# Attention and a gated feed-forward layer in one kernel: unit pairs in the first weight groups, a split fourth group, and work moved from the vector engine to ScalarE at the start

## The chip, the cores and the metric

The kernel runs on one core of a Trainium2 chip. The metric is the device time of one execution in microseconds. A "slow" or "quick" execution below is a long or short one.

Names that come back: TensorE multiplies matrices (PE in the profile, its weight loads are PEld), the vector engine is DVE, ScalarE is ACT, GpSimd is POOL, and SP issues most of the DMA transfers (95 of 103 in the profile of before, ScalarE the rest).

## The reference

Inputs are `q`, `k`, `v` of shape (8 batches, 8 heads, 576 rows, 64), `w_in` (512 x 2048), `w_out` (2048 x 512) and `beta` (2048).

```python
q_s = softmax(q, axis=-1)              # over the 64 columns
k_s = softmax(k, axis=2)               # over the 576 rows
kv  = einsum('bhsd,bhse->bhde', k_s, v)
x   = einsum('bhsd,bhde->bhse', q_s, kv)   # then heads side by side: 4608 x 512
h   = x @ w_in                         # 4608 x 2048
g   = h / (1 + exp(-beta * h))
out = g @ w_out                        # 4608 x 512
```

## The kernel before

The 4608 rows are worked off in nine slabs of 512: slabs 0 to 7 are the first 512 rows of a batch each, and slab 8 is gathered from the remaining 64 rows of all batches. A slab has two passes. Pass 1 makes 16 hidden units of 128 columns, each from four matmuls over the input pieces `m`; ScalarE applies Silu. Pass 2 multiplies by the output weights. The short K-V matmuls of the next batch stand between them.

At the start everything comes in at once: q, k, v, then the input weights in four column groups of 512 (`c`), then the output weights in the same staging buffers. The input weights are cast to bf16; the output weights are scaled by 1/beta. In a group of four units, unit `f` takes every fourth column:

```python
HB = (0, 1, 2); OB = (3, 4); MB = (5, 6, 7)          # PSUM banks
def pass1_mm(t, f, m, bk):
    ...
    l = bass.AP(WIN, m * DFF + 512 * (f // 4) + f % 4, [[NM * DFF, 128], [4, 128]])
    mm(PS[bk][:, :], l, x[:, m, :], m == 0, m == NM - 1, ...)
    if m == NM - 1: ...  # Silu on ScalarE: GT[:, f, :]
# ... slab 0
FIRST = (12, 5)
at = by_m(0, 0, 4); ...                    # units 0-3, then 4-7, 8-11: input piece outermost
for g in (4, 8):
    at = by_m(0, g, g + 4)
    for m in range(NM):
        at(m)
for e_ in range(2):
    homes_ek(1, e_, [("win", 2, NM - 1)])  # GpSimd zeroes batch 1's key buffer after group 2's last cast
# ... units 12-15 follow one by one, each needing all four pieces
```

Batch 1's attention is done inside pass 2 of slab 0, at places counted in matmuls:

```python
todo = [(107, lambda: go(t_steps(1, (0, 1), (1,)))),     # transposes, QT copied by the vector engine
        (112, lambda: go(t_steps(1, (2, 3), (2,)))),
        (112.1, lambda: scale_wout(14, 2)),
        (115, lambda: kv_mm(1, 0, 0, 0, D + 1)), (117, kv1),   # ends in KVD, on the vector engine
        (122, lambda: out_now(1, 0, 7, DVE)), ...]             # TensorE needs KVD and QT here
...
exp_q(1, 0, 2); norm_main(1, 0, 1); norm_main(1, 1, 1, POOL); scale_wout(8); exp_q(1, 2, 2); ...
```

The remaining rows of a pair of batches (`QRF`) are loaded with the odd batch, normalised, and turned by a transposing DMA into `QTR`; both are issued by SP. For slabs 2 and up pass 1 cycles through three banks (`HB[f % 3]`).

```python
def load(b):
    load_main("qf", ...); load_k(b); load_v(b)
    if b % 2: load_qrem(b - 1)             # batch 3 brings the remaining rows of batches 2 and 3
# slab 0's end: store(0); load(3)
# slab 1, after pass 1: exp_qr(0); norm_rem(0); tr_dma(0)   -> QTR for batches 0 and 1
# slab 1, pass 2, place 101.5 on: outr_steps(1)             -> TensorE needs QTR
```

The softmax here doesn't subtract the row's maximum and nothing guards it: scores larger than these inputs give would overflow.

## Time and profile before

| | before |
|---|---|
| timed, first three executions | 285.06, 285.56, 286.23 us |
| the profiled execution | 286.38 us, span 284.6 us |
| TensorE busy | 277.9 us, 98% |
| vector engine, ScalarE, GpSimd | 42%, 62%, 14% |

TensorE is busy almost throughout, so only its holes can be saved. The first part of the page has the busy times (share of the span, instructions):

```profile
PE 277.9 (98%) x1585; PEld 138.7 (49%) x1585; DVE 120.3 (42%) x220; ACT 176.3 (62%) x240; POOL 39.0 (14%) x58
```

The timeline of TensorE shows the holes. Its columns are start, length, engine, source line, operation, output and inputs, sizes and count, and in brackets an idle time with what ended it. Most matmuls come from one helper, L366, so the tile names tell them apart.

```profile
13.80 1.02 PE L366 MATMUL PS<-XT,WIN 128*128 128x512 bf16 x4
...
15.53 9.49 PE L366 MATMUL PS<-XT,WIN 128*128 128x512 bf16 x43
25.52 3.66 PE L366 MATMUL PS<-XT,WIN 128*128 128x512 bf16 x15 [0.50 <-DVE WIN L564]
29.02 9.44 PE L366 MATMUL PS<-WOUT,GT 128*128 128x512 bf16 x43
...
41.92 1.24 PE L366 MATMUL PS<-WOUT,GT 128*128 128x512 bf16 x5
44.03 0.39 PE L366 MATMUL PS<-QT,KVD 128*128 128x512 bf16 x1 [0.87 <-DVE KVD L403]
...
60.81 8.37 PE L366 MATMUL PS<-WOUT,GT 128*128 128x512 bf16 x38
69.01 0.25 PE L366 MATMUL PS<-QTR,KVD 128*128 128x64 bf16 x3
```

Matmuls of 512 columns start every 0.216 us where nothing is missing (43 in 9.28 us from 29.02). Between 13.80 and 29.02 there are 66 of them, 14.25 us of work in 15.22 us: hole 1. Five matmuls from 41.92 should hand over at 43.0, but the next one starts at 44.03: hole 2. The brackets alone understate both, because the modelled end of a matmul (0.38 us after its start) overlaps the start of the next one (0.216 us after it). Hole 2 ends with KVD; on the timeline of the vector engine:

```profile
43.36 0.61 DVE L403 TENSOR_TENSOR KVD<-PS,RC 64x128 bf16<-64x128 f32 x2
```

The timeline of the vector engine and of GpSimd shows what makes hole 1: the casts of the fourth group and the memset lie on top of each other. The first line is the end of the third group's casts, which the memset waits for.

```profile
21.96 0.76 DVE L564 CAST WIN<-O2S 128x512 bf16<-128x512 f32 x2 [0.59 <-DMA O2S<-in_moe_w_in_dram]
23.31 2.82 DVE L564 CAST WIN<-O2S 128x512 bf16<-128x512 f32 x4 [0.58 <-DMA O2S<-in_moe_w_in_dram]
22.85 2.33 POOL L236 MEMSET EK<- 64x1152 f32 x2 [6.74 <-DVE WIN L564]
```

The same timeline in a narrower window shows one of those four casts by itself, 1.36 us long:

```profile
24.10 1.36 DVE L564 CAST WIN<-O2S 128x512 bf16<-128x512 f32 x1
```

### The profile page before, as it was taken

The numbers are of one execution on the slowest core, as the hardware profiler recorded it, in microseconds if no ns is written. First come the engines' busy times: TensorE is split into PE (matmuls) and PEld (weight loads), VectorE is DVE, ScalarE is ACT, GpSimd is POOL, SyncE is SP. The second block draws the span as 40 slices with busy tenths as digits, with TensorE's granted clock in tenths as the row PEclk, the third lists the DMA queues.
The fourth block names the chain that finished last, engine by engine and source line by source line (L and its number), as shares of the span: only waits on it lengthen the run. The fifth ranks groups of instructions, "written<-read, shape, count | busy, mean of one in ns | idle before, by whom it ended". The sixth has DMA issues, their size and how long they took to land.

```text
span 284.6 us, 3906 instructions
## 1 busy us (share of the span) xinstructions
PE 277.9 (98%) x1585; PEld 138.7 (49%) x1585; DVE 120.3 (42%) x220; ACT 176.3 (62%) x240; POOL 39.0 (14%) x58
## 2 busy tenths in 40 slices
PE   7899998999999999999999999999999999999995
PEld 3554454445555445544554455444554455445443
DVE  4866797109881248114741564054704300110012
ACT  5977656889977935796479737892660086018500
POOL 6623141306212032100130000000000000000000
PEclk9999999999999999999999999999999999999999
DMA  7999999995998999207980033001600030002022
GB/s 246 371 391 406 391 386 379 325 387 101 281 388 211 377 346 318 57 15 234 379 131 1 0 150 74 0 3 79 160 2 0 0 147 2 0 39 111 0 68 79
DMA packets 41210, 50.07 MB, mean 176 GB/s; under 512 B 20324, under 2 KB 28772, under 8 KB 39784
## 3 DMA queue, kind: packets, MB, share of 16 engines
q1 hardware_dynamic: 40240, 48.77, 53.2%
q10 hardware_dynamic: 952, 1.06, 1.3%
q8 instruction: 12, 0.20, 0.3%
q14 instruction: 6, 0.05, 0.1%
HBM read 36.71 MB, written 9.44 MB: 162 GB/s over the span
## 4 chain that ended last, share of the span: by engine, by line
PE 85%; DVE 5%; DMA 4%; SPq 3%; ACT 1%; issue 0%
PE PS L366 85%; DMA O2S<-in_moe_w_in_dram 4%; DVE WOUT L553 2%; SPq L560 2%; SPq L259 1%; DVE QS L332 1%; DVE WIN L564 1%; DVE EQ L334 1%; ACT L295 0%; DVE QT L384 0%; SPq L249 0%; DVE QI L333 0%; ACT GT L637 0%; ACT EQ L295 0%; DVE KVD L403 0%
## 5 line engine op out<-in xcount | busy, mean ns | idle before, releaser
L637 ACT ACTIVATE GT<-PS,BETA 128x512 bf16<-128x512 f32 x144 | 96.8, 688 | 78.5 <-PE PS L366 78.3
L366 PE MATMUL PS<-XT,WIN 128*128 128x512 bf16 x576 | 133.3, 380 | 0.6 <-DVE WIN L564 0.5
L366 PE MATMUL PS<-WOUT,GT 128*128 128x512 bf16 (+2 forms) x592 | 132.8, 373 | 0.0
L366 PEld LDWEIGHTS PS<-XT,WIN 128*128 128x128 bf16 x576 | 64.4, 113 | 57.8 <-DVE WIN L564 1.4
L366 PEld LDWEIGHTS PS<-WOUT,GT 128*128 128x128 bf16 x592 | 55.2, 98 | 62.0 <-DVE WOUT L553 0.3
L704 DVE COPY O2S<-PS 128x512 f32<-128x512 f32 x33 | 22.7, 687 | 107.7 <-PE PS L366 107.7
L366 PE MATMUL PS<-VB,EK 128*128 128x65 bf16 (+2 forms) x306 | 35.8, 192 | 0.7 <-POOL VB L351 0.4
L351 POOL CAST VB<-VF 128x576 bf16<-128x576 f32 x31 | 23.1, 747 | 75.0 <-DMA VF<-in_v_dram 37.3
L307 ACT ACTIVATE EK<-KF 64x1152 bf16<-64x1152 f32 x24 | 27.8, 1158 | 0.4
L366 PEld LDWEIGHTS PS<-VB,EK 128*128 128x128 bf16 x306 | 22.5, 99 | 8.0 <-POOL VB L351 1.0
L332 DVE TENSOR_REDUCE QS<-EQ 128x8 f32<-128x512 bf16 (+1 forms) x22 | 20.1, 914 | 3.6 <-ACT EQ L295 3.5
L441 DVE CAST XT<-PS 128x512 bf16<-128x512 f32 x24 | 16.4, 690 | 10.9 <-PE PS L366 10.9
L295 ACT ACTIVATE EQ<-QF 128x512 bf16<-128x512 f32 x32 | 17.8, 618 | 2.4 <-DMA QF<-in_q_dram 2.2
L334 DVE TENSOR_TENSOR EQ<-EQ,QI 128x1024 bf16<-128x1024 bf16 (+1 forms) x15 | 16.6, 1104 | 0.5
L366 PE MATMUL PS<-QT,KVD 128*128 128x512 bf16 x32 | 12.2, 380 | 0.9 <-DVE KVD L403 0.9
L317 ACT ACTIVATE EK<-KF 64x576 bf16<-64x576 f32 (+1 forms) x12 | 10.0, 840 | 4.0 <-DMA KF<-in_k_dram 3.9
L334 POOL TENSOR_TENSOR EQ<-EQ,QI 128x512 bf16<-128x512 bf16 x7 | 7.4, 1051 | 23.3 <-DVE QI L333 23.1
L403 DVE TENSOR_TENSOR KVD<-PS,RC 64x64 bf16<-64x64 f32 (+2 forms) x28 | 8.6, 308 | 1.7 <-PE PS L364 0.8
L366 PE MATMUL PS<-XT 128*128 128x512 f32 x10 | 7.5, 883 | 1.5 <-DVE XT L219 1.5
L340 DVE TENSOR_REDUCE QRS<-EQR 128x8 f32<-128x512 bf16 x4 | 2.7, 681 | 13.2 <-ACT EQR L322 13.2
L637 ACT ACT_TABLE_LOAD x5 | 6.4, 1283 | 0.1
L295 ACT ACT_TABLE_LOAD x5 | 6.4, 1283 | 0.1
(51 smaller groups left out, 77.8 us busy)
## 6 DMA issues: line engine op xcount, KB each, us to landing
out_dram<-O2S SPq DMA_DIRECT2D x8, 1024.0 KB, 4.9
KF<-in_k_dram SPq DMA_DIRECT2D x6, 1152.0 KB, 8.5
VF<-in_v_dram SPq DMA_DIRECT2D x6, 1152.0 KB, 11.3
QF<-in_q_dram SPq DMA_DIRECT2D x6, 1024.0 KB, 7.1
KF<-in_k_dram SPq DMA_DIRECT2D x8, 288.0 KB, 8.0
VF<-in_v_dram SPq DMA_DIRECT2D x8, 288.0 KB, 8.8
WST<-in_moe_w_in_dram SPq DMA_DIRECT2D x8, 256.0 KB, 8.1
O2S<-in_moe_w_in_dram SPq DMA_DIRECT2D x4, 512.0 KB, 12.0
```

Source lines behind the costliest of these rows:

```text
L295: add(ACTE, lambda e, o=o, a=a: e.activation(o, a, ACT.Exp), r=[("qf", i, hp)], w=[("eq", i, hp)])
L307: add(ACTE, lambda e, o=o, a=a: e.activation(o, a, ACT.Exp), r=[("kf", i, h) for h in hps], w=[("ek", i, h, e_) for h in hps])
L317: add(ACTE, lambda e: e.activation(o, a, ACT.Exp), r=[("kf", i, h) for h in hps], w=[("ek", i, h, e_) for h in hps])
L332: add(DVE, lambda e: e.tensor_reduce(s_, a, AX.X, ALU.add), r=ks, w=[("qs", i, hp0)])
L334: add(eng, lambda e: e.tensor_tensor(a, a, vb, ALU.mult), r=ks + [("qi", i, hp0)], w=ks)
L351: add(eng, lambda e: (e.copy if eng == ACTE else e.tensor_copy)(o, a), r=[("vf", i, hp), ("vone", i)], w=[("vb", i, hp, h) for h in ((0, 1 ...
L366: add(PE, lambda e: e.matmul(o, l, r_, start=start, stop=stop), r=r, w=w, bank=[bk])
L403: add(DVE, lambda e, o=o, a=a, s_=s_: e.tensor_tensor(o, a, s_, ALU.mult), r=[("ps", bk)] + [("rc", i, h) for h in hps], w=[("kvd", i, h, ...
L441: add(eng, lambda e: (e.copy if eng == ACTE else e.tensor_copy)(XT[i][:, hp, :], PS[bk][:, :]), r=[("ps", bk)], w=[("xt", i, hp)], bank=[bk])
L553: add(DVE, lambda e, f=f: e.tensor_scalar(WOUT[:, f, :], STAGE[f // 4][:, f % 4, :], RB[:, f:f + 1], None, ALU.mult), r=[SKEY[f // 4][f % ...
L637: add(ACTE, lambda e: e.activation(GT[:, f, :], PS[bk][:, :], ACT.Silu, scale=BETA[:, f:f + 1]), r=[("ps", bk), "beta"], w=[("gt", f)], ba ...
L704: add(eng, lambda e: (e.copy if eng == ACTE else e.tensor_copy)(O2S[t % 2][:, u, :], PS[bk][:, :]), r=[("ps", bk)], w=[("o2", t % 2, u)], ...
```

## The change

The intent: close hole 1 by taking the fourth group in pairs of units with the input piece outermost, and by zeroing the key buffer later; close hole 2 by moving two QT copies (and one value cast) to ScalarE; scale the third output-weight group earlier, since TensorE will ask for it earlier; and let the first eight units take every second column instead of every fourth. The core of the diff:

```diff
+            if f < 8:       # load_wout: rows in pairs, to match
+                a = bass.AP(wout_h, 512 * c * DM, [[2 * DM, 128], [256 * DM, 2], [1, 2 * DM]])
+                o = bass.AP(STAGE[c], 0, [[4 * DM, 128], [2 * DM, 2], [1, 2 * DM]])
...          # turn_beta: 8 small transposes instead of 4, to match
-            l = bass.AP(WIN, m * DFF + 512 * (f // 4) + f % 4, [[NM * DFF, 128], [4, 128]])
+            n = 2 if f < 8 else 4
+            l = bass.AP(WIN, m * DFF + 128 * (f // n * n) + f % n, [[NM * DFF, 128], [n, 128]])
...
-        FIRST = (12, 5)
+        FIRST = (16, 5)
...          # head: one input cast from GpSimd to the vector engine, outputs 2 and 3 swap engines
-        for g in (4, 8):
-            at = by_m(0, g, g + 4)
+        for g, n in ((4, 4), (8, 4), (12, 2), (14, 2)):
+            at = by_m(0, g, g + n)
...
-            homes_ek(1, e_, [("win", 2, NM - 1)])
+            homes_ek(1, e_, [("win", 3, NM - 1)])
...
-                todo = [(107, lambda: go(t_steps(1, (0, 1), (1,)))),
-                        (112, lambda: go(t_steps(1, (2, 3), (2,)))),
-                        (112.1, lambda: scale_wout(14, 2)),
+                todo = [(107, lambda: go(t_steps(1, (0, 1), (1,), ACTE))),
+                        (112, lambda: go(t_steps(1, (2, 3), (2,), ACTE))),
+                        (112.1, lambda: (scale_wout(14, 2), exp_kh(1, 2, 1, 0), exp_kh(1, 2, 1, 1))),
...
+                scale_wout(8)
                 norm_main(1, 1, 1, POOL)
-                scale_wout(8)
...
-                    cast_v(1, hp)
+                    cast_v(1, hp, POOL if hp else ACTE)
```

More of the change, by code (lines that the diff above doesn't have):

```diff
@@ L536, in go @@
                 s()
-        load_v(0, 4)
         STAGE = (WST[0], WST[1], O2S[1], O2S[0])
@@ L546, in load_wout @@
             c, x = f // 4, f % 4
-            a = bass.AP(wout_h, (512 * c + x) * DM, [[4 * DM, 128], [1, n * DM]])
-            o = bass.AP(STAGE[c], x * DM, [[4 * DM, 128], [1, n * DM]])
+            if f < 8:
+                a = bass.AP(wout_h, 512 * c * DM, [[2 * DM, 128], [256 * DM, 2], [1, 2 * DM]])
+                o = bass.AP(STAGE[c], 0, [[4 * DM, 128], [2 * DM, 2], [1, 2 * DM]])
+            else:
+                a = bass.AP(wout_h, (512 * c + x) * DM, [[4 * DM, 128], [1, n * DM]])
+                o = bass.AP(STAGE[c], x * DM, [[4 * DM, 128], [1, n * DM]])
             add(SP, lambda e: e.dma_start(o, a), w=SKEY[c][x:x + n], slot=f"wst{f}")
@@ L569, in turn_beta @@
         def turn_beta():
-            for k_ in range(4):
-                mm(bass.AP(PS[KB], 16 + k_, [[512, 128], [4, 4]]),
-                   bass.AP(BT, k_, [[512, 4], [4, 128]]), IDF[0:4, 0:4],
-                   True, True, r=["bt", "idf"], w=[("ps", KB)], bk=KB, tr=True)
+            for g, n, o in ((4, 4, 0), (2, 2, 0), (2, 2, 256)):
+                for k_ in range(n):
+                    mm(bass.AP(PS[KB], 16 + o // 128 + k_, [[512, 128], [4, g]]),
+                       bass.AP(BT, o + k_, [[512, g], [n, 128]]), IDF[0:g, 0:g],
+                       True, True, r=["bt", "idf"], w=[("ps", KB)], bk=KB, tr=True)
         def read_beta():
@@ L606, in bass_efficient_attn_shen__then__act_swish_beta_kernel @@
         ksum(0, 0, KB)
+        load_v(0, 4)
         for c in range(4):
@@ L613, in bass_efficient_attn_shen__then__act_swish_beta_kernel @@
         cast_v(0, 3)
-        for m in range(1, NM):
-            cast_win(0, m, POOL)
+        cast_win(0, 2, POOL)
+        cast_win(0, 3, POOL)
+        cast_win(1, 0, POOL)
         warm(1, 0, True)
@@ L625, in bass_efficient_attn_shen__then__act_swish_beta_kernel @@
         kvd(0, 1, 1, 0)
-        cast_win(0, 0, DVE)
         orot = [0]
@@ L656, in pass1_tile @@
                 tick()
-        FIRST = (12, 5)
+        FIRST = (16, 5)
         out_now(0, 0, 0, ACTE)
+        cast_win(0, 0, DVE)
         kv_mm(0, 2, 7, 0, D + 1)
@@ L662, in bass_efficient_attn_shen__then__act_swish_beta_kernel @@
         kvd(0, 2, 7, 0)
+        cast_win(0, 1, DVE)
         out_now(0, 1, 6, ACTE)
+        at = by_m(0, 0, 4)
         kv_mm(0, 3, 1, 0, D + 1)
+        at(0)
+        out_now(0, 2, 0, ACTE)
         ksum_inv(0, 1, 3, 1, D, 1)
         kvd(0, 3, 1, 0)
-        at = by_m(0, 0, 4)
-        at(0)
-        out_now(0, 2, 0, DVE)
-        at(1, 0, 2)
-        out_now(0, 3, 7, ACTE)
-        at(1, 2)
+        at(1)
+        out_now(0, 3, 7, DVE)
         read_beta()
@@ L678, in bass_efficient_attn_shen__then__act_swish_beta_kernel @@
         for c in range(1, 4):
-            for m in range(NM):
+            for m in range(1 if c == 1 else 0, NM):
                 cast_win(c, m, DVE)
@@ L808, in bass_efficient_attn_shen__then__act_swish_beta_kernel @@
                 exp_kh(1, 0, 2, 1)
-                exp_kh(1, 2, 1, 0)
-                exp_kh(1, 2, 1, 1)
                 norm_main(1, 2, 1, POOL)
```

## The prediction

> **What bounds it now.** TensorE: busy 277.9 of 284.6 us in the profile; 512-column matmuls start every 0.216 us where the timeline is dense (43 in 9.28 us from 29.02). The chain of waits is TensorE alone from 44.03 on. So only TensorE's holes can be saved. After the head (13.8 us) the timeline and the weight-load view show two:
> - Fourth input-weight group, 24.8 to 26.2. From 13.80 to 29.02 there are 66 matmuls, 14.25 us of work in 15.22: 0.97 us lost. Unit 12 needs all four input pieces first, and the vector engine's casts are late: one took 1.36 us instead of 0.42 beside GpSimd's memset of batch 1's key buffer (1.22 us). [...]
> - Batch 1's first output: matmuls resume at 44.03 for a KVD released at 43.98, about 1.0 us lost. The vector engine is busy 9.3 of the 10 us from 30 to 40, and on up to KVD.
>
> DMA is over 90% busy from 3 to 60 us at some 390 GB/s, so loads will not land earlier.
>
> **What the change does.**
> - Fourth group by pairs of units, input outermost: the pieces are wanted at about 24.6, 25.0, 25.5 and 25.9 instead of all within 0.86 us. The memset moves behind the last cast. Estimate: the hole closes, -0.9 us.
> - Two QT copies (1.27 us) leave the vector engine, in the second hole's chain; ScalarE waits 2.5 us for key data before 41.54, so has room. Third-group scales go ahead of batch 1's second normalization: needed, because TensorE would want unit 8 near 34.9, one us earlier. Those weights land near 33.6, so the vector engine may sit 0.7 us, and that normalization is some 1.7 us later; the transposes (wanted near 37.3) and the unit-12 scale (near 39.3) become marginal: up to 0.4 us of new waits. Estimate: KVD near 42.1 instead of 43.98; with the first hole, -1.4 to -1.9 us.
> - First eight units in pairs: column step 2 instead of 4. Weight loads take 113 ns against 98 for unit-step output weights, but hide under 216 ns matmuls: 0. Output-weight loads in 4 KB instead of 8 KB pieces: 0 to +0.2 us in landing, with 0.5 us to spare.
> - Head: one input cast moves from GpSimd to the vector engine, outputs 2 and 3 swap engines, four more small beta transposes: about 0; the pieces' landings (13.2, 13.9, ...) pace it.
>
> Later stages are dense and shift rigidly; ScalarE's exponentials at 62 to 79 us follow, their data having landed.
>
> **Prediction.** 284.0 us against 285.56, range 283.1 to 285.2. Faster by over 2%: 0.01; within 2%: 0.975; slower by over 2%: 0.015.
>
> **What would show it.**
> - First hole: fourth-group casts 0.42 us each, no TensorE wait for WIN, output matmuls starting near 28.1 instead of 29.0.
> - Second: KVD and the first batch-1 output near 42.1, TensorE's wait for KVD under 0.3 us; QT copies about 1 us each on ScalarE, nobody waiting.
> - New waits, if any: transposes on EQ from GpSimd, or unit 12 on WOUT, each under 0.4 us.
> - Pairs: matmul interval unchanged.
>
> **What would make it wrong.** Weights landing later than estimated; the second normalization delaying the transposes by over 1 us; GpSimd casts blocking the fourth scales; ScalarE's added 2.7 us delaying the key exponentials of pair 2, so that the gap moves instead of closing; run-to-run spread (1.2 us before).

The sum came to 284.0 us, 1.56 us under 285.56: -1.4 to -1.9 us for the two holes, 0 for the pairs, 0 to +0.2 us for the landing of the output weights, about 0 for the head. The landing term was the author's estimate and rested on no trace of before; afterwards the two loads in 4 KB pieces landed 11.0 and 11.2 us after their issue in after, beside 11.0 and 11.0 us in before.

## The result, and the profile after

The changed kernel took 285.16 us (median of 6, 284.96 to 285.39) beside 285.35 us for the one before (6 executions, 284.78 to 286.23). The ratio is 0.9992, with a 95% interval of 0.9975 to 1.0009: the same. Ratios are the mean time of one kernel's fast runs over that of the other's of the same rounds, so not quite the ratio of the medians quoted.

The two profiles say something else: the span went from 284.6 to 283.1 us. The profiled execution of before was 286.38 us, slower than all six timed ones; that of after was 284.96 us, its quickest.

Here are the lines of after that answer to those of before: the busy times of the page, then the timeline of TensorE, then that of the vector engine, GpSimd and ScalarE.

```profile
PE 275.2 (97%) x1559; PEld 136.0 (48%) x1589; DVE 117.3 (41%) x218; ACT 178.6 (63%) x243; POOL 38.6 (14%) x57
```

```profile
13.77 1.02 PE L366 MATMUL PS<-XT,WIN 128*128 128x512 bf16 x4
...
28.20 9.44 PE L366 MATMUL PS<-WOUT,GT 128*128 128x512 bf16 x42
...
42.38 0.38 PE L366 MATMUL PS<-QT,KVD 128*128 128x512 bf16 x1
...
59.15 8.36 PE L366 MATMUL PS<-WOUT,GT 128*128 128x512 bf16 x37
68.08 0.26 PE L366 MATMUL PS<-QTR,KVD 128*128 128x64 bf16 x3 [0.57 <-DMA QTR<-EQR]
```

```profile
16.14 0.69 DVE L530 CAST XT<-PS 128x512 bf16<-128x512 f32 x1 [0.64 <-PE PS L366]
...
23.19 0.76 DVE L566 CAST WIN<-O2S 128x512 bf16<-128x512 f32 x2 [0.58 <-DMA O2S<-in_moe_w_in_dram]
24.55 0.76 DVE L566 CAST WIN<-O2S 128x512 bf16<-128x512 f32 x2 [0.60 <-DMA O2S<-in_moe_w_in_dram]
...
41.63 0.61 DVE L403 TENSOR_TENSOR KVD<-PS,RC 64x128 bf16<-64x128 f32 x2
25.43 2.17 POOL L236 MEMSET EK<- 64x1152 f32 x2 [8.68 <-DVE WIN L566]
...
39.74 1.92 ACT L384 COPY QT<-PS 128x1024 bf16<-128x1024 bf16 x2
```

The two holes are closed, but for 0.11 us before batch 1's first output: the casts of the fourth group take 0.43 us each and nobody waits for them, and KVD is done at 42.24 instead of 43.97. A small hole is new, 0.18 us at 16.6. Because outputs 2 and 3 swapped engines, the last input piece of slab 0 is now cast out of PSUM by the vector engine, until 16.83; TensorE could take it up at 16.81 and does so at 16.98. All nine traces of kernels with the changed head show this hole, none of the nine without it. Pass 2 of slab 1 begins 1.66 us earlier (59.15 against 60.81). But nine microseconds later TensorE waits, where it did not before, for the transposing DMA of QTR; only 0.93 us of the 1.66 are left at that point. (Some 30 matmul records are missing in this trace, 1559 against 1589 weight loads; a missing one of 512 columns shows as one start-to-start distance of 0.43 us and is no hole.)

Both traces hold every weight load, so the Nth load from the end can be compared in all of them. The table gives, for each execution that was profiled, its own time and the start of the weight load at four places: the first of slab 0's pass 2 (after hole 1), the first of slab 1's pass 2 (after both holes), the first of slab 2's pass 1 (after QTR), and the last of all. The last column is the distance from the second place to the last.

| execution | its time | slab 0 pass 2 | slab 1 pass 2 | slab 2 pass 1 | last | from slab 1 pass 2 to the last |
|---|---|---|---|---|---|---|
| before | 286.38 | 28.80 | 60.60 | 76.64 | 281.30 | 220.70 |
| before_1 | 284.98 | 28.14 | 59.17 | 75.22 | 279.89 | 220.72 |
| before_2 | 285.43 | 27.86 | 59.58 | 75.63 | 280.31 | 220.73 |
| before_3 | 285.28 | 28.07 | 59.46 | 75.50 | 280.18 | 220.72 |
| before_4 | 286.11 | 28.92 | 60.30 | 76.34 | 281.02 | 220.72 |
| before_5 | 286.64 | 29.06 | 60.85 | 76.90 | 281.56 | 220.71 |
| after | 284.96 | 28.00 | 58.94 | 75.72 | 279.87 | 220.93 |
| after_1 | 284.70 | 27.95 | 58.87 | 75.46 | 279.61 | 220.74 |
| after_2 | 285.04 | 28.02 | 58.93 | 75.81 | 279.96 | 221.03 |
| group4_only | 285.76 | 28.21 | 59.95 | 76.00 | 280.69 | 220.74 |
| act_only | 285.32 | 28.67 | 59.52 | 75.57 | 280.25 | 220.73 |
| pairs_only | 284.71 | 28.07 | 59.31 | 75.36 | 279.62 | 220.31 |
| after_nopairs | 284.73 | 28.07 | 58.92 | 74.97 | 279.66 | 220.74 |
| after_banks | 284.17 | 28.00 | 58.85 | 74.93 | 279.08 | 220.23 |
| qr_late | 284.58 | 28.21 | 59.02 | 75.06 | 279.46 | 220.44 |
| qr_late_2 | 284.44 | 28.07 | 58.92 | 74.97 | 279.37 | 220.45 |
| qr_late_banks | 284.28 | 28.14 | 58.99 | 75.03 | 279.18 | 220.19 |
| qr_late_banks_2 | 284.38 | 28.23 | 59.13 | 75.17 | 279.32 | 220.19 |

Read it by columns. Before runs the last 220.7 us alike to 0.03 us in all six executions; whatever distinguishes a quick execution from a slow one happens before 60 us.

### The profile page after: what moved, and what is told of

The parts are those of the page before. It is cut to its first block, busy times and chain, and to the rows that moved or that the text cites. A ratio compares the mean times of both kernels' runs of the same rounds, so it can differ in the third digit from the quotient of the medians.

```text
span 283.1 us, 3884 instructions
## 1 busy us (share of the span) xinstructions
PE 275.2 (97%) x1559; PEld 136.0 (48%) x1589; DVE 117.3 (41%) x218; ACT 178.6 (63%) x243; POOL 38.6 (14%) x57
## 3 DMA queue, kind: packets, MB, share of 16 engines
q10 hardware_dynamic: 952, 1.06, 1.1%
## 4 chain that ended last, share of the span: by engine, by line
PE 90%; ACT 4%; DMA 3%; issue 1%; DVE 1%; SPq 0%; ACTq 0%
PE PS L366 89%; ACT EK L317 2%; DMA KF<-in_k_dram 2%; DMA QTR<-EQR 2%; ACT L322 0%; SPq L249 0%; PE PS L364 0%; ACT GT L642 0%; DVE QRS L340 0%; DVE EQR L343 0%; ACT VB L351 0%; ACT EQR L322 0%; ACT XT L530 0%; ACT O2S L710 0%; DVE O2S L731 0%
## 5 line engine op out<-in xcount | busy, mean ns | idle before, releaser
L366 PE MATMUL PS<-WOUT,GT 128*128 128x512 bf16 (+2 forms) x579 | 131.4, 373 | 0.7 <-issue 0.2
L366 PE MATMUL PS<-XT,WIN 128*128 128x512 bf16 x561 | 131.2, 379 | 0.5
L366 PEld LDWEIGHTS PS<-XT,WIN 128*128 128x128 bf16 x576 | 60.1, 106 | 59.3 <-POOL WIN L566 0.5
L366 PE MATMUL PS<-QT,KVD 128*128 128x512 bf16 x30 | 11.4, 379 | 0.0
L366 PE MATMUL PS<-XT 128*128 128x512 f32 x10 | 6.7, 801 | 1.5 <-DVE XT L219 1.5
```

The costliest lines, as they stand in the source:

```text
L366: add(PE, lambda e: e.matmul(o, l, r_, start=start, stop=stop), r=r, w=w, bank=[bk])
```

## The experiments

Theories after the first comparison: (A) the profile of before was of a slow execution, so its holes are larger than usual; (B) the holes are constant, and the gain is lost elsewhere. For what came back at 68 us: QTR is held up by loads queued ahead of it, or the wait is chance.

### before_1, before_2, before_3: the kernel before, unchanged, profiled again

No edit.

> The kernel before, unchanged, profiled again. Its first profile is of an execution of 286.4 us, slower than five of its six timed ones (284.8 to 286.2). Theory A (the first profile was a poor baseline): this profile has a shorter span, near 283.6 us, the sum of the holes at 24.6 us (0.9 us) and at 42.8 us (1.0 us) is smaller by 0.5 us or more, and the pair transpose of batches 0 and 1 (QTR) lands again near 67.9 us. Theory B (the first profile is typical, the holes are constant, and the change's gain is lost in what the profile does not show): span 284.4 to 284.8 and both holes as before.

> A second look at the same kernel, for the spread: A expects the holes to differ between executions by several tenths of a us with the landings of the loads; B expects them alike within 0.1 us.

> The kernel before, a fourth profile, for its spread: the end of the execution (285 to 286.6 us) should follow the sum of its holes before 60 us within 0.2 us, and from 61 us on its matmuls should be spaced as in the other three within 0.05 us.

They took 284.98, 285.43 and 285.28 us. In matmul starts, what exceeds 0.213 us per matmul adds up to this: hole 1 was 0.91 us in the first profile and 0.25, 0 and 0.19 us in these; hole 2 was 1.04 us and then 0.28, 0.68 and 0.63 us. All three began slab 1's pass 2 1.0 to 1.4 us earlier than the first profile. Theory A holds, B falls. In before_1 the third group's casts were done earlier, and so the memset ran earlier relative to the fourth group's:

```profile
21.13 0.76 DVE L564 CAST WIN<-O2S 128x512 bf16<-128x512 f32 x2 [0.59 <-DMA O2S<-in_moe_w_in_dram]
22.02 2.17 POOL L236 MEMSET EK<- 64x1152 f32 x2 [5.62 <-DVE WIN L564]
23.28 2.18 DVE L564 CAST WIN<-O2S 128x512 bf16<-128x512 f32 x4 [1.39 <-DMA O2S<-in_moe_w_in_dram]
```

There the memset ended at 24.2, so that one cast was long (1.18 us) and the others were done by 25.5; in the first profile the second memset started at 23.96 and the next cast, from 24.10, lasted until 25.46. All four casts together took 2.18 us in before_1 and 2.80 to 2.82 us in the three slow profiles of before. With no memset beside it a cast took 0.42 us (before, at 22.30) or 0.43 us (qr_late, at 24.76); one memset took 1.22 us beside the casts (before, before_5) and 1.06 us without them (after). Why both are longer side by side no trace shows. How late the memset runs goes with a landing: the last load of the third group landed at 21.94, 22.06 and 22.20 us in the three slow profiles of before (two of them came later, see below) and at 20.62 to 21.12 us in the three quick ones, while the first load of the fourth group landed at 23.0 to 23.6 us in all six. Why that load is late in some executions stays open, and so does what makes hole 2 vary. The expected QTR landing "again near 67.9 us" was a miss: it landed at 67.2 to 67.5 us here.

### after_1 and qr_late: is the QTR wait chance, and what is it worth?

after_1 is the changed kernel, unchanged. qr_late issues the remaining-row loads of batches 2 and 3 after the transposes:

```diff
-            if b % 2:
+            if b % 2 and b != 3:
                 load_qrem(b - 1)
...
-                if b % 2 == 1:
+                if b % 2 == 1 and b != 3:
                     exp_qr(b // 2)
...
                     for hp in range(NHP):
                         cast_v(3, hp)
+                    load_qrem(2)
+                    exp_qr(1)
                     load(4)
```

> The changed kernel, profiled and timed again. All theories: 284.9 to 285.4 us. The theory of the DMA cap expects TensorE to wait again 0.5 to 0.9 us for the transpose QTR, which lands at 67.8 to 68.2 us, just after the last of the remainder-query loads of batches 2 and 3; a theory that this wait was chance expects under 0.2 us.

> The changed kernel with the remainder-query loads of batches 2 and 3 issued after the transposes of batch 2 instead of before the transpose QTR, and their exponential after the key exponentials. DMA cap theory: QTR lands before 67 us, TensorE no longer waits for it, and the median falls by 0.5 to 0.8 us to about 284.4. Rival (the transpose itself takes 4 us beside any traffic, or the wait moves to the next DMA in line): QTR lands 4 us after its issue as before, or as much is lost within the next 10 us; median unchanged within 0.2 us.

after_1: 284.80 us (284.69 to 285.21) beside 285.37 us; ratio 0.9968 (0.9941 to 0.9996). The QTR wait came again, 0.54 us by matmul starts, 0.73 us in the first profile of after.

qr_late: 284.76 us (284.55 to 285.24), ratio 0.9969 (0.9939 to 0.9999). The wait for QTR is gone, and QTR lands 2.5 us after its issue instead of 4.3. The tile view of QTR tells it, first for after, then for qr_late:

```profile
L456 SPq DMA_TRANSPOSE QTR<-EQR x1: 1292/1292/1292, 63.7 to 63.7; - x1
...
DMA to landing us min/median/max: 4.3/4.3/4.3
```

```profile
L456 SPq DMA_TRANSPOSE QTR<-EQR x1: 1301/1301/1301, 63.8 to 63.8; - x1
...
DMA to landing us min/median/max: 2.5/2.5/2.5
```

The order of landings in the other traces fits. The second of the two remaining-row loads landed at 66.66, 67.30, 67.24 and 67.47 us in before_1, before, after_1 and after; QTR followed at 67.2, 67.8, 67.7 and 68.0 us, whether it was issued at 63.6 or at 65.4. QTR ended 0.5 to 0.6 us after the loads that SP had issued ahead of it, 2.5 to 4.4 us after its own issue. So in these traces its landing goes with those loads, not with TensorE, and qr_late shows that they are what holds it up: there it landed at 66.3 us with the loads moved, and in the four traces with them moved it took 2.5 to 3.0 us. By what means they hold it up was not shown. TensorE wants QTR 3.66 us after its issue.

The expected fall of the median by 0.5 to 0.8 us did not come: it was 0.04 us. In the profile a gap of 0.24 us stood at 78 us (in the traces of before there is one of 0.1 us at the same unit), and there was some loss in executions that were not profiled. The timeline of qr_late at 77 us:

```profile
75.60 0.63 ACT L322 ACTIVATE EQR<-QRF 128x512 bf16<-128x512 f32 x1
76.25 1.28 ACT L642 ACT_TABLE_LOAD   x1
77.54 2.63 ACT L642 ACTIVATE GT<-PS,BETA 128x512 bf16<-128x512 f32 x4
77.77 0.38 PE L366 MATMUL PS<-XT,WIN 128*128 128x512 bf16 x1
77.99 0.23 PE L366 MATMUL PS<-VB,EK 128*128 128x65 bf16 x2
78.29 0.39 PE L366 MATMUL PS<-XT,WIN 128*128 128x512 bf16 x1
```

ScalarE is at its exponentials until 76.2 and at a table load of 1.28 us after them, and its first Silu of slab 2 begins only at 77.54. TensorE has by then filled three banks; unit 3 has to wait for the first bank to be read, and the matmul at 78.29 is 0.24 us late (with two more banks the gap went, see qr_late_banks).

### group4_only, act_only, pairs_only: one part of the change each, on the kernel before

group4_only has `FIRST = (16, 5)`, the loop over `((4, 4), (8, 4), (12, 2), (14, 2))` and the memset after `("win", 3, NM - 1)`. act_only has the `todo` lines, the order of `scale_wout(8)` and the value cast. pairs_only has `load_wout`, `turn_beta` and the column step. All as in the diff above.

> The kernel before with the fourth input-weight group by pairs and the key-buffer memset behind it, alone. Theory: the casts of the fourth group take 0.43 us each, no hole at 24 to 26 us, so that the output matmuls start within 14.4 us of the first input-weight matmul; what is gained is then mostly given back at the KVD hole of 42 us, which depends on the vector engine and on landings. Median 0 to 0.4 us under before, and the executions over 286 us become rarer, as a long cast behind the memset is one source of them. Rival (the holes depend on data landings alone): the hole before the output matmuls stays.

> The kernel before with the ScalarE part alone (two QT copies and one value cast on ScalarE, third output-weight group scaled first). Theory: the hole before batch 1's first output shrinks to under 0.3 us, that at 24 to 26 us stays and varies; the slab then arrives at the transpose QTR about as early as in the quick executions of before, with a wait of 0 to 0.4 us there. Median 0.1 to 0.5 us under before. Rival (ScalarE becomes the limit): ScalarE's key exponentials of pair 2 end later than 43 us and TensorE waits for EK.

> The kernel before with the column pairs alone (first eight units, their output weights and betas). Comparing traces by matmul index, after gained 0.08 us on before in the first half of each of the slabs 2 to 6, only where short K-V matmuls stand between the input-weight matmuls: 0.5 us in all. Theory of the weight load (a shorter column step makes the load quicker, and it is exposed there): this kernel shows the same 0.07 to 0.19 us per slab, 0.4 to 0.5 us from 76 us to the end, and a median about 0.4 us under that of before. The prediction's theory (hidden, 0): no drift beyond 0.05 us in all.

One chip, before 285.46 us (11 executions, 284.92 to 286.65):

| | median us | lowest to highest | ratio (95%) | hole 1 | hole 2 |
|---|---|---|---|---|---|
| group4_only | 285.50 | 285.31 to 285.76 | 0.9993 (0.9976 to 1.0009) | 0 | 0.68 us |
| act_only | 285.43 | 285.26 to 286.27 | 0.9993 (0.9975 to 1.0011) | 0.78 us | 0.11 us |
| pairs_only | 285.11 | 284.71 to 285.92 | 0.9985 (0.9965 to 1.0005) | 0.26 us | 0.49 us |

The first two each close the hole that they are meant to close, and neither moves the median. With hole 1 closed alone, TensorE is done with batch 1's transposes earlier and meets the vector engine there: it waits 0.2 us at 39.6 for output weights that are still being scaled (until 39.82), then 0.68 us for KVD. The profiled execution of group4_only also started 0.4 us late in the head.

pairs_only gave what had been predicted as nothing: from slab 1's pass 2 to the end it takes 220.31 us, 0.41 less than all six profiles of before. The weight-load groups of before, then of pairs_only, over the whole run (count, busy us, mean ns):

```profile
L366 PEld LDWEIGHTS PS<-XT,WIN 128*128 128x128 bf16 x576 | 64.4, 113 | 57.8 <-DVE WIN L564 1.4 <-issue 0.8 <-ACT GT L637 0.4
```

```profile
L366 PEld LDWEIGHTS PS<-XT,WIN 128*128 128x128 bf16 x576 | 60.1, 106 | 59.5 <-DVE WIN L568 0.7 <-ACT GT L643 0.4 <-issue 0.3
```

The mean of 106 ns is made of 98 ns for units 0 to 7, now with a column step of 2, and 113 ns for the rest, still with 4; the loads of pass 2 also take 98 ns (they load the hidden units `GT` with a step of 1, not the output weights as the prediction has it). Between 90 and 200 us the distance between two input-weight matmuls was 216.0 ns on average in both, so there a single load hides either way; from an input-weight matmul to a K-V matmul after it, it was 219.6 ns in before and 217.0 ns in pairs_only. An estimate of the reason, from these means: two loads fall into one matmul of 216 ns there, 98 + 113 = 211 ns against 98 + 98. The traces show the distances, not this cause. The K-V matmuls of a batch stand beside units 2 to 8 of pass 1, at some 27 places a slab (96 between 90 and 200 us, 3.5 slabs): 27 x 2.6 ns is 0.07 us a slab, in five slabs 0.35 us. The table shows 0.41 us, 0.07 to 0.09 in each slab. The trace of pairs_only holds its own control: there the distance is 216.4 ns on average after units up to 7 (step 2, 91 places) and 221.1 ns after unit 8 (still step 4, 12 places). So it is the column step, and not the new order of the output weights or of beta.

### qr_late_banks: both later waits taken away

qr_late, and two more banks for pass 1 of slab 2, banks 3 and 4, which pass 2 uses and which are free then:

```diff
-        HFIRST = ((3, 4, 5, 6, 0, 1, 7, 2, 3, 4, 5, 6, 0, 1, 7, 2), (2, 1, 3, 4, 5, 6, 0, 7))
+        HFIRST = ((3, 4, 5, 6, 0, 1, 7, 2, 3, 4, 5, 6, 0, 1, 7, 2), (2, 1, 3, 4, 5, 6, 0, 7),
+                  (0, 1, 2, 3, 4, 0, 1, 2, 3, 4, 0, 1, 2, 0, 1, 2))
...
-            return HFIRST[t][f] if t < 2 and f < len(HFIRST[t]) else HB[f % 3]
+            return HFIRST[t][f] if t < 3 and f < len(HFIRST[t]) else HB[f % 3]
```

> The late remainder-query loads, and two more PSUM banks for the first units of slab 2, so that TensorE need not wait there for ScalarE, whose exponentials run until 77.5 us. With the loads late, the wait for QTR went (0.5 to 0.7 us), but the median fell by only 0.04 us, and a gap of 0.24 us stood at 78.0 us. Theory (the next limit is ScalarE's exponentials through three banks): no gap at 78 us, last matmul 0.2 to 0.3 us earlier than in the late-load kernel, median 284.2 to 284.6. Rival (the late-load kernel's gain is lost in executions that were not profiled, elsewhere): median unchanged at 284.7 to 284.9.

284.23 us, and all six executions between 284.14 and 284.28; ratio 0.9946 (0.9930 to 0.9962). The gap at 78 us is gone and the distance to the end is 220.19 us. The expectation held in the median, and the narrow spread was not expected: 0.14 us, where the 11 executions of before spread over 1.7 us on the same chip.

### after_nopairs and after_banks: what remains without the pairs, and with the banks alone

after_nopairs sets the three tests of the pairs back (`f < 0`, `((4, 4, 0),)`, `n = 4`); after_banks is the changed kernel with the two `HFIRST` lines alone.

> The changed kernel without the column pairs (both holes and the head as in the change). Theory of the sum: before's quick executions are only 0.25 to 0.65 us behind at 59 us and the QTR wait takes 0.5 to 0.75 us back; the 0.4 us of after come from the pairs. Then this kernel has no drift in slabs 2 to 6, waits for QTR as after does, and its median is 0.3 to 0.5 us over that of after, 285.1 to 285.4, within 0.3 us of before. Rival (the holes are the gain): median within 0.15 us of after.

> The changed kernel with the two more banks in slab 2 alone, the remainder-query loads where they were. Theory: the QTR wait comes first and hides ScalarE's; it stays 0.4 to 0.8 us, and the median stays within 0.25 us of after (284.7 to 285.1). Rival (banks are what gained in the last kernel): median 284.2 to 284.4.

> The late-load kernel again, one look. Its timed executions fell in two groups, 284.6 to 284.8 and 285.1 to 285.2; the one profiled was of the first. If this is of the second, theory: the extra 0.5 us stand at 77 to 79 us, where TensorE waits for a bank that ScalarE has not read; the rival: in the first 60 us. If of the first group, the gap at 78 us is 0.2 to 0.3 us again.

Beside a before of 286.15 us (284.94 to 287.46; many slow executions of it), after_nopairs took 285.47 us (284.73 to 285.72), ratio 0.9988 (0.9968 to 1.0008), and after_banks 285.01 us (284.17 to 285.60), ratio 0.9977 (0.9955 to 0.9999). The order is as the sum wants it, but the profiles missed the expectation in one point: in both, QTR landed at 67.2 us and nobody waited for it. Those two profiled executions were the quickest of their six, 284.73 and 284.17 us, and the others took up to 1.0 and 1.4 us more. So the QTR wait differs from execution to execution, from none to the 0.8 us seen in after_2, and the banks without the late loads do not bring the narrow spread. That the slower executions of after_banks are slow by QTR is likely, since qr_late_banks differs from it by the late loads alone and has no such spread, but no profile caught one of them. For after_nopairs it is open: qr_late, which does not wait for QTR either, has executions 0.5 us slower than its quickest.

qr_late_2 was of the quick group again (284.44 us, the gap at 78 us again 0.24 us). Why two of six executions of qr_late took 285.1 to 285.2 us stays open; with more banks none did.

### before_4, before_5, after_2, qr_late_banks_2: slow executions, and the best version on one chip

No new edits.

> The kernel before, a fifth profile. The misjudged baseline rests on one slow profile (286.4 us) against three of 285.0 to 285.4. Theory: whatever its time, the time less 285.0 us equals its holes before 60 us less those of the first repeat, within 0.2 us, and the slow ones have the long hole at 24 to 26 us and the KVD hole of 0.6 us or more together. Rival: a slow execution is slow after 60 us (clock, or a wait there).

> A sixth profile of before, with the same expectations: the theory ties its time to its holes before 60 us within 0.2 us, the rival finds a slow execution slow after 60 us.

> The changed kernel, timed beside the best version on one chip: 284.7 to 285.4 us, with a QTR wait between 0 and 0.8 us in the profile.

> The late loads with two more banks, again, beside after and before on one chip: 284.1 to 284.4 us with a spread under 0.3 us, 0.5 to 1.0 us under after; no wait for QTR and none at 78 us.

Both looks at before caught slow executions, 286.11 and 286.64 us. They are slow through the two holes: 0.91 and 0.63 us in before_4, 1.13 and 1.03 us in before_5, and alike afterwards (220.72 and 220.71 us in the table). The third group lands late and the casts lie under the memset again, as in the first profile. Here are before_5's waits of TensorE (total us, times, longest), and then the timeline of its casts and memset:

```profile
PE PS L366 <- DVE KVD L403: 0.9, 1, 0.9
PE PS L366 <- DVE WIN L564: 0.7, 1, 0.7
```

```profile
23.58 2.80 DVE L564 CAST WIN<-O2S 128x512 bf16<-128x512 f32 x4 [0.59 <-DMA O2S<-in_moe_w_in_dram]
23.11 2.33 POOL L236 MEMSET EK<- 64x1152 f32 x2 [7.01 <-DVE WIN L564]
```

Against before_1 the time of these two is longer by 1.13 and 1.66 us, their two holes by 1.0 and 1.6 us, and slab 1's pass 2 starts later by 1.13 and 1.68 us. The rival (slow after 60 us) falls.

On the same chip, before took 285.57 us (284.83 to 286.70), after_2 285.43 us (284.90 to 285.59; ratio 0.9984, 0.9968 to 1.0000) and qr_late_banks_2 284.30 us (284.16 to 284.57; ratio 0.9948, 0.9932 to 0.9964). The profile of after_2 waits for QTR once more, that of qr_late_banks_2 has the same place without a wait. TensorE of the two:

```profile
59.15 8.37 PE L366 MATMUL PS<-WOUT,GT 128*128 128x512 bf16 x37
68.17 0.26 PE L366 MATMUL PS<-QTR,KVD 128*128 128x64 bf16 x3 [0.65 <-DMA QTR<-EQR]
```

```profile
59.34 8.37 PE L366 MATMUL PS<-WOUT,GT 128*128 128x512 bf16 x37
67.54 0.25 PE L366 MATMUL PS<-QTR,KVD 128*128 128x64 bf16 x3
```

The first is 9.02 us apart, the second 8.20 us. The expectation of 0.5 to 1.0 us under after was a little short: it is 1.13 us by the medians. The spread was 0.41 us, over the expected 0.3: one execution took 284.57 us, the rest 284.16 to 284.38.

## Why the prediction was right or wrong

It forecast 284.0 us, 1.56 us less; the medians of three sets fell by 0.19, 0.57 and 0.14 us. "Within 2%" was right, and the mechanism at the start was right, but not the size of the holes that it was taken off, nor what it said of the later stages.

- **The first 60 us: right against the profile.** Casts of 0.43 us and no wait for WIN; output matmuls from 28.20 (predicted "near 28.1"); KVD done at 42.24 and the first batch-1 output at 42.38 ("near 42.1"); QT copies of 1.0 us each with nobody waiting; 1.66 us gained at 59 us ("-1.4 to -1.9 us").
- **The baseline of that sum: wrong.** The term "0.97 us lost" for the first hole and "about 1.0 us lost" for the second were read from one execution of 286.38 us, and the sum was taken off a median of 285.56 us. In the three quicker profiles of before the holes add up to 0.5, 0.7 and 0.8 us, and against those executions after is ahead at slab 1's pass 2 by only 0.2 to 0.7 us (59.17, 59.58 and 59.46 against 58.94 and 58.87). The profile's own time stood beside it and would have shown this.
- **"Head: ... about 0": wrong by 0.18 us**, the wait for the last input piece at 16.6. From the first input-weight matmul to slab 0's pass 2 after takes 14.43 us in each of its three traces, and the quick executions of before take 14.53, 14.26 and 14.45: against them the first hole brought nothing, and the lead at 59 us comes from the second hole (0.4 us) and a start of pass 1 that is 0.1 us earlier (13.70 against 13.82 in the mean).
- **"Later stages are dense and shift rigidly; ScalarE's exponentials at 62 to 79 us follow, their data having landed": wrong for the one step that TensorE reaches by DMA.** QTR is released by TensorE's progress but lands behind SP's bulk loads, at 67.2 to 68.0 us in these traces. The three profiles of after waited 0.73, 0.54 and 0.82 us for it. The prediction had read "DMA is over 90% busy from 3 to 60 us" as a limit on loads and did not ask which later transfer lands behind them.
- **"Weight loads ... hide under 216 ns matmuls: 0": wrong.** The pairs gave 0.41 us from slab 2 on, shown by pairs_only, at the places where a short K-V matmul follows. It is the only part that after keeps against quick executions of before.
- **Of the possible failures that it named**, "run-to-run spread (1.2 us before)" was the right one, but as a mere blur; the spread was in fact the holes themselves coming and going. "GpSimd casts blocking the fourth scales" did not come: in before two of these scales had taken 1.68 us beside GpSimd's casts (from 39.18), as long as four of the second group's without them (from 29.71), but in after the two from 39.01 took 0.87 us and the next two 0.49 us each.

Put together, with the table: at slab 1's pass 2, after's three profiles are 1.08 us ahead of the mean of the six of before (59.99 against 58.91), lose 0.54 to 0.82 us at QTR, and win 0.52 us from slab 2 on: 0.41 us by the pairs, and 0.1 us because TensorE, held up at QTR, no longer meets the wait at 78 us, which the traces of before and of pairs_only have and those of after do not. That gives 0.90 us (1.08 - 0.70 + 0.52) against a mean that includes three slow executions of six, and 0.31 us against the mean of the three quick ones (59.40 - 58.91 = 0.49, - 0.70 + 0.52), which is the order of what the medians show. The last weight loads in the table are apart by as much, 0.90 and 0.31 us.

## What to carry to other kernels

Compare the profiled execution's own time with the timed median before taking a hole's length as a gain; where a hole depends on which of two engines starts first, profile several executions (hole 1 was 0 to 1.13 us in the six of before). When an engine is made quicker in a stretch where DMA is busy throughout (here over 90% from 3 to 60 us), follow the transfers that it releases later: here a small one landed only 0.5 to 0.6 us after the bulk loads issued ahead of it, and its consumer waited 0.54 to 0.82 us. The gain reached the median only after two later waits had been removed too; with them gone the spread was 0.14 and 0.41 us (6 executions each), where before had 1.7 and 1.9 us (11 each) on the same chips.
